# Ending the held-back weight portions earlier, and copying first partial sums by ScalarE

## The chip, the cores and the metric

One core of one Trainium2 chip runs the whole program. The metric is device time in microseconds (us) of one execution. A core has five engines, each with its own instruction queue that it works off in order: PE (TensorE, matrix products; PEld is its weight load), DVE (VectorE), ACT (ScalarE), POOL (GpSimd) and SP (SyncE, which here issues all DMAs). SBUF is the working memory, PSUM the small memory into which PE accumulates.

## The reference

Three layers follow one another. The last two are multilayer perceptrons over 2304 tokens:

```
scores = 0.125 * q @ k^T          # 4 batches, 8 heads, 576 positions, head size 64
attn   = softmax(scores where 0 <= i - j < 64)
x      = attn @ v                 # 2304 x 512
g      = x @ w_gate               # 512 x 1536
y      = (g * sigmoid(g) * (x @ w_val)) @ w_out         # 1536 x 512
h      = y @ w_in                 # 512 x 2048
out    = max(0.01 * h, h) @ w_out2                      # 2048 x 512
```

Attention, y and out are float32, the weights come as float64. The kernel multiplies in float32r with every operand split into a high and a low part, so each product is three matmuls (high*high, high*low, low*high).

## The kernel before

The first perceptron is done in six blocks of tokens (BLOCKS). Block 0 takes 24 steps, blocks 1 to 5 take 12 steps each, one for each of the 12 portions of 128 columns of d_ff. A step (`step1`, L558) is three slots long and makes twelve matmuls for the gate (pg), twelve for the value (pv) and twelve for the output of the step before (acc, in `out1`, L533). Blocks 1 to 4 have 320 tokens, block 5 has 512. FIRST holds the first slot of each block: block 1 starts at slot 72, block 5 at 216, and END is 252. The attention of each block is worked in small pieces during the block before. A slot is also the unit of priority: `prio(slot)` sets the priority of what is emitted next, and a scheduler with a cost model then puts each engine's instructions in an order, which is fixed when the program is built.

The second perceptron is a Strassen-Winograd scheme of seven products (A11, A12, S1 to S4, A22). It needs each weight portion, and four sums of parts, split into high and low. `ready2(fp)` (L319) and `ready2o(fp)` (L332) prepare one of eight portions of w_in and w_out2: two loads of 512 KB through `narrow` (L263), four sums on DVE, and four stores by `keep2` (L309) to DRAM, with two more stores at the very last portion (plain, L345). That is 16 conversions, and the list todo2 (L604) says at which slot each is emitted; the loop at L610 does so at the first step whose slot has reached it, with priority slot + 4. Of the two loads, each waits for a mark: `wait_for_mark` (L259) is a POOL instruction that copies one element of the newest g (or, later, of c) into the load's target, so that the DMA can't start earlier. All targets and stores of conversions, and the loads of x2 (below), go through one ring of three buffers (rawp).

In block 5 the kernel also builds the split right factors of the second perceptron's first pass (`x2_part`, `finish_x2`, L615 to 620) from y in DRAM, and fetches the split weights of units 0 and 1 (`fetch_a`, L623). They go into the places of weight portions that block 5 no longer needs.

The second perceptron has three passes of 768 tokens, eight units each (L751). A unit makes seven products of six matmuls each into three PSUM tiles pw, px, py (`product`, L637). ACT copies or applies the leaky function (L780, L793, L769), DVE adds (L785, L815, L826, L845, L831 to L849), POOL adds once (L816), and `halves` (L655) splits each result by an ACT cast and a POOL subtraction. The tiles t1, t5 and c lie where the first perceptron kept th and g (L775), and pw, py and px where it kept pg, pv and the attention's scores. Between the products PE makes the y matmuls of the unit before (`part_y`, L682). Their partial sums leave PSUM by `add` (L674): in the first unit of a pass by a copy (L677), in the seven others by an addition on DVE (L679). `y1`, `y2` and `y3` use the same PSUM bank one after the other, so the copy of y1 must be done before y2 can write. At the end of a pass `finish` adds the sums up and stores them from the place into which the next pass copies.

Of the kernel before, what the change touches and what calls it, by code (L numbers as in the profile page):

```python
# [22 lines left out]
def f32(ap):  # L23
    return ap.bitcast(F32)
# [3 lines left out]
def banded_attention_moe_moe(  # L28
# [12 lines left out]
    nc = tc.nc  # L41
# [17 lines left out]
    NP2 = NF2 // 2  # L59
# [19 lines left out]
    def prio(slot):  # L79

        tc.cur_priority = int(1000 * (slot + 100))
# [385 lines left out]
    for n, j in enumerate(jobs):  # L467
# [16 lines left out]
        i = n - min(jj.n for jj in jobs if jj.blk == j.blk)  # L484
# [116 lines left out]

    END = FIRST[NBLK]
    begin2, last2 = FIRST[1] + 20, FIRST[NBLK - 1]
    todo2 = [begin2 + (last2 - begin2) * i / 10 for i in range(10)] + [last2 + 3 + 5 * i for i in range(6)]  # L604
    todo2 = [(at_, (ready2, ready2o)[i % 2], i // 2) for i, at_ in enumerate(todo2)]
    for blk in range(1, NBLK):
        for f in range(NF1):
            slot = FIRST[blk] + 3 * f
            step1(slot, blk, slice(0, WIDTH[blk]), f, f == 0, f == NF1 - 1)
            while todo2 and slot >= todo2[0][0]:  # L610
                prio(slot + 4)
                _, fn, i = todo2.pop(0)
# [54 lines left out]
    def sums(r):  # L667
        return (space[10][:, 1280 * r:1280 * r + 1280] if r < 2 else space[11][:, 0:1280]).rearrange(
            "p (k n) -> p k n", k=5)

    def sums1():
        return space[11][:, 1280:2816].rearrange("p (k r n) -> p k r n", k=2, r=3)

    def add(dst, ps, first):  # L674
        prio(slot - 3)
        if first:
            nc.vector.tensor_copy(f32(dst), ps)  # L677
        else:
            nc.vector.tensor_tensor(f32(dst), ps, f32(dst), op=ALU.add)  # L679
        prio(slot)  # L680

    def part_y(n, ps, k, r, start):  # L682
        g = G[n, k]
        for m, (a, b) in enumerate(((0, 0), (0, 1), (1, 0))):
            nc.tensor.matmul(ps, lhsT=g[:, a, r * P:r * P + P], rhs=O2[n, k][:, b], start=start and m == 0,  # L685
                             stop=m == 2, skip_group_check=True)

    yb, yc = {}, {}

    def y1(n, r):  # L690
        yb[r] = ps_acc.tile([P, 2, 256], F32, tag=f"acc{r}", name="y")
        part_y(n, yb[r][:, 0], S2, r, True)
        part_y(n, yb[r][:, 1], A11, r, False)
        add(sums(r)[:, 0:2], yb[r], n % NP2 == 0)

    def y2(n, r):
        part_y(n, yb[r][:, 0], S3, r, False)
        part_y(n, yb[r][:, 1], A12, r, False)
        add(sums(r)[:, 2:4], yb[r], n % NP2 == 0)

    def y3(n, r):
        part_y(n, yb[r][:, 0], A22, r, False)
        add(sums(r)[:, 4], yb[r][:, 0], n % NP2 == 0)

    def y4(n, rs, last):
        if not last:
            yc[rs] = (ps_acc if len(rs) > 1 else ps_att).tile([P, 2, 256], F32, tag="acc3" if len(rs) > 1 else "att",
                                                              name="yc")
        for j, r in enumerate(rs):
            part_y(n, yc[rs][:, j], S4 if last else S1, r, not last and j == 0)  # L710
        add(sums1()[:, int(last), rs[0]:rs[-1] + 1], yc[rs][:, 0:len(rs)], n % NP2 == 0)

    def total(r):

# [36 lines left out]
    for n, (i, fp) in enumerate(units):  # L751
# [45 lines left out]
        for r in range(3):  # L797
            y(y1, r)
# [20 lines left out]
        y(y2, 2)  # L819
        new_o(A22, S4)  # L820
        y(y4, (0, 1), False)
        y(y4, (2,), False)
        step()
        product(n, py, S4, False)
# [23 lines left out]
        if n < LAST:  # L848
            nc.vector.tensor_tensor(t["t1"], t["t1"], t["c"], op=ALU.subtract)  # L849
            halves(n, S4, t["t1"])  # L850
        y(y4, (0, 1), True)
        y(y4, (2,), True)
        if n and (e == 0 or n == LAST):
# [34 lines left out]
```

## Time and profile before

| | |
|---|---|
| Three runs | 972.27, 975.13 and 977.71 us, median 975.13 |
| Profiled execution | 970.93 us, span 969.0 us |
| PE busy | 925.0 us (95% of the span) |
| DVE, ACT, POOL busy | 662.6, 469.0 and 336.4 us |
| Mean granted clock | 0.979 |
| Mean DMA rate | 182 GB/s, 59.0% of 16 engines' span on the main queue |

How to read it: the span is from the first to the last instruction. A busy time counts only the instructions themselves. The granted clock is the share of TensorE's full clock that the throttle allowed; 1.00 is 2.4 GHz and 0.5 is 1.2 GHz. In a list of instructions in order of time the columns are the start, the length, the engine, the line, the operation, and in square brackets the idle time of that engine just before and what ended it. Attention and block 0 fill the first 121 us, blocks 1 to 4 run to about 478 us, block 5 to about 578 us, and the rest is the second perceptron.

### The profile page before, as it was taken

Reading aid. Unit: us, or ns where it says so; the run is one execution under the profiler, and the core shown is the slowest. Engines: PE = TensorE matmul, PEld = TensorE weight load, DVE = VectorE, ACT = ScalarE, POOL = GpSimd, SP = SyncE. Lnnn points to the kernel's source line nnn. Section 1 sums busy time; section 2 is a strip of 40 time slices with the busy share of each in tenths; the row PEclk is TensorE's granted clock in tenths of the full one; section 3 lists DMA queues with packets and bytes.
Section 4 is the critical chain, followed back from the end, with each engine's and each line's share of the span. In section 5 each row is a group of like instructions: output and inputs, shape, how many; then the busy total and the mean of one; then the engine's idle time right before and its main releaser. Section 6 shows DMA issues by size and latency. Waiting matters only on the chain.

```text
span 969.0 us, 18774 instructions
## 1 busy us (share of the span) xinstructions
PE 925.0 (95%) x6573; PEld 881.5 (91%) x6573; DVE 662.6 (68%) x1554; ACT 469.0 (48%) x1194; POOL 336.4 (35%) x402
## 2 busy tenths in 40 slices
PE   8898999999999999999999984799999999999998
PEld 6788999999999999999988873799999999999997
DVE  5788842336556565665445664898998999879887
ACT  6976633335545554666333433444544445334441
POOL 1012231111111111111122121666667666576554
PEclk8999999999999999999999996899999999999999
DMA  8777621225654564554346858778557875587742
GB/s 208 220 205 226 182 43 29 74 43 157 182 163 131 140 191 131 167 155 148 112 158 231 317 188 284 269 249 261 169 184 231 262 251 165 154 252 244 252 159 83
DMA packets 193901, 176.09 MB, mean 182 GB/s; under 512 B 114576, under 2 KB 142224, under 8 KB 193808
## 3 DMA queue, kind: packets, MB, share of 16 engines
q1 hardware_dynamic: 193808, 174.90, 59.0%
q8 instruction: 52, 0.85, 0.4%
q14 instruction: 41, 0.34, 0.1%
HBM read 135.00 MB, written 39.85 MB: 180 GB/s over the span
## 4 chain that ended last, share of the span: by engine, by line
PE 73%; DMA 11%; DVE 8%; issue 2%; ACT 2%; SPq 2%; POOL 1%; POOLq 0%; DVEq 0%; ACTq 0%
PE pg L526 12%; PE y L685 12%; PE pv L526 12%; PE acc L526 12%; PE px L642 7%; PE yc L685 5%; DMA raw<-in_moe_w_gate_dram 4%; PE pw L642 4%; PE py L642 4%; PE s L202 2%; PE pv L244 2%; DMA raw<-in_moe_w_out_dram 1%; DVE u L275 1%; PE pt L233 1%; DMA raw<-in_moe_w_in_dram 1%
## 5 line engine op out<-in xcount | busy, mean ns | idle before, releaser
L579 POOL TENSOR_TENSOR g<-th,g 128x320 fp32r<-128x320 f32 (+2 forms) x84 | 81.5, 970 | 434.9 <-ACT g L578 423.3
L526 PE MATMUL pg<-x,w 128*128 128x320 f32 (+2 forms) x1008 | 175.2, 321 | 8.2 <-DVE th L569 5.2
L526 PE MATMUL pv<-x,w 128*128 128x320 f32 (+2 forms) x1008 | 174.5, 320 | 1.8 <-DVE st L219 1.2
L526 PE MATMUL acc<-g,w 128*128 128x320 f32 (+2 forms) x1008 | 170.7, 316 | 0.1
L526 PEld LDWEIGHTS pg<-x,w 128*128 128x128 f32 x1008 | 150.5, 191 | 17.0 <-DVE th L569 6.4
L526 PEld LDWEIGHTS pv<-x,w 128*128 128x128 f32 x1008 | 151.9, 192 | 9.2 <-ACT th L568 1.5
L526 PEld LDWEIGHTS acc<-g,w 128*128 128x128 f32 x1008 | 150.1, 189 | 7.0 <-POOL g L579 0.7
L685 PE MATMUL y<-space,g 128*128 128x256 f32 x1035 | 147.5, 283 | 1.0 <-DVE space L677 0.7
L685 PEld LDWEIGHTS y<-space,g 128*128 128x128 f32 x1035 | 138.3, 190 | 2.8 <-DVE space L679 1.0
L679 DVE TENSOR_TENSOR space<-y,space 128x512 f32<-128x512 f32 (+1 forms) x180 | 102.8, 593 | 11.4 <-PE y L685 10.4
L569 DVE SCALAR_TENSOR_TENSOR th<-th,pg 128x320 f32<-128x320 f32 (+2 forms) x84 | 41.3, 492 | 93.6 <-ACT th L568 93.4
L642 PE MATMUL px<-space,space 128*128 128x384 f32 x432 | 91.7, 344 | 8.2 <-DVE u L815 7.2
L664 POOL TENSOR_TENSOR g<-t,g 128x384 fp32r<-128x384 f32 x71 | 77.3, 1090 | 53.0 <-ACT g L663 48.8
L642 PEld LDWEIGHTS px<-space,space 128*128 128x128 f32 x432 | 76.3, 194 | 9.6 <-DVE u L815 7.8
L642 PE MATMUL py<-space,space 128*128 128x384 f32 x288 | 66.8, 347 | 10.1 <-ACT c L769 8.5
L578 ACT CAST g<-th 128x320 fp32r<-128x320 f32 (+2 forms) x84 | 39.1, 466 | 63.9 <-DVE th L576 63.3
L568 ACT ACTIVATE th<-pg 128x320 f32<-128x320 f32 (+2 forms) x84 | 37.0, 441 | 65.2 <-PE pg L526 63.5
L685 PE MATMUL yc<-space,g 128*128 128x256 f32 x414 | 65.0, 282 | 2.7 <-DVE space L677 2.7
L642 PE MATMUL pw<-space,space 128*128 128x384 f32 x288 | 64.7, 341 | 2.4 <-ACT c L769 1.8
L273 ACT ACTIVATE u<-raw 128x512 f32<-128x512 f32 x68 | 46.1, 682 | 41.5 <-DMA raw<-in_moe_w_out_dram 18.1
L274 DVE TENSOR_SCALAR raw<-raw 128x512 int32<-128x512 int32 x68 | 31.6, 466 | 47.9 <-DMA raw<-in_moe_w_out_dram 20.3
L664 POOL TENSOR_TENSOR g<-c,g 128x384 fp32r<-128x384 f32 x47 | 50.6, 1077 | 39.7 <-ACT g L663 29.2
(141 smaller groups left out, 1474.4 us busy)
## 6 DMA issues: line engine op xcount, KB each, us to landing
space<-o SPq DMA_DIRECT2D x147, 256.0 KB, 3.4
space<-a SPq DMA_DIRECT2D x140, 256.0 KB, 3.4
raw<-in_moe_w_out_dram SPq DMA_DIRECT2D x28, 512.0 KB, 4.3
a<-hl SPq DMA_DIRECT2D x24, 512.0 KB, 3.0
o<-hl SPq DMA_DIRECT2D x24, 512.0 KB, 2.8
raw<-in_moe_w_in_dram SPq DMA_DIRECT2D x16, 512.0 KB, 4.8
raw<-in_moe_w_gate_dram SPq DMA_DIRECT2D x12, 512.0 KB, 5.2
raw<-in_moe_w_val_dram SPq DMA_DIRECT2D x12, 512.0 KB, 4.6
```

What stands on the lines that cost most here:

```text
L202: nc.tensor.matmul(ps[:, a], lhsT=qbd[:, t, :], rhs=kT[:, w0:w0 + P], start=True, stop=True)
L273: nc.scalar.activation(u, f32(high), AF.Prelu, scale=EXP_SCALE, alpha=NEGATIVE)
L274: nc.vector.tensor_single_scalar(low, low, 29, op=ALU.logical_shift_right)
L526: nc.tensor.matmul(ps, lhsT=w(a, c), rhs=x(b, c), start=(start and n == 0), stop=(stop and n == 3 * len(cs) - 1), skip_group_check=True)
L568: nc.scalar.activation(th, pg, AF.Tanh, scale=0.5)
L569: nc.vector.scalar_tensor_tensor(out=th, in0=th, scalar=1.0, in1=pg, op0=ALU.add, op1=ALU.mult)
L578: nc.scalar.copy(g[0][:, :n], th)
L579: nc.gpsimd.tensor_tensor(g[1][:, :n], th, f32(g[0][:, :n]), op=ALU.subtract)
L642: nc.tensor.matmul(ps, lhsT=A2[n, k][:, a, c * P:c * P + P], rhs=X2[i, c, k][:, b], start=start and m == 0, stop=m == 5, skip_group_check= ...
L664: (lo or nc.gpsimd).tensor_tensor(g[:, 1], src, f32(g[:, 0]), op=ALU.subtract)
L679: nc.vector.tensor_tensor(f32(dst), ps, f32(dst), op=ALU.add)
L685: nc.tensor.matmul(ps, lhsT=g[:, a, r * P:r * P + P], rhs=O2[n, k][:, b], start=start and m == 0, stop=m == 2, skip_group_check=True)
```

## The change

Two edits. The first spreads the 16 conversions at equal distances: the step between two is 124/14 = 8.86 slots where it was 12.4 for the first ten and 5 for the last six, and the last two are due at slots 216 and 224.86 where they were due at 239 and 244. The second makes the copies of `y1` and of both `y4` calls, in the first unit of a pass, on ScalarE in place of VectorE; those of `y2` and `y3`, and all additions, stay.

```diff
     begin2, last2 = FIRST[1] + 20, FIRST[NBLK - 1]
-    todo2 = [begin2 + (last2 - begin2) * i / 10 for i in range(10)] + [last2 + 3 + 5 * i for i in range(6)]
+    todo2 = [begin2 + (last2 - begin2) * i / 14 for i in range(16)]
...
-    def add(dst, ps, first):
+    def add(dst, ps, first, copy=nc.vector.tensor_copy):
         prio(slot - 3)
         if first:
-            nc.vector.tensor_copy(f32(dst), ps)
+            copy(f32(dst), ps)
...
-        add(sums(r)[:, 0:2], yb[r], n % NP2 == 0)
+        add(sums(r)[:, 0:2], yb[r], n % NP2 == 0, nc.scalar.copy)
...
-        add(sums1()[:, int(last), rs[0]:rs[-1] + 1], yc[rs][:, 0:len(rs)], n % NP2 == 0)
+        add(sums1()[:, int(last), rs[0]:rs[-1] + 1], yc[rs][:, 0:len(rs)], n % NP2 == 0,
+            nc.scalar.copy)
```

## Rows read from the trace of the kernel before

**Rows 1.** Busy time of each engine by stretch (start and end, length, busy us and count of PE, PEld, DVE, ACT and POOL, then granted clock, DMA share, GB/s). The stretches are blocks 1 to 4 with conversions, block 5, the change to the second perceptron, the starts of passes 2 and 3, and the end.

```profile
215.00:478.00 263.00, 262.62 (x2007) 256.42 (x2006) 152.12 (x481) 142.12 (x423) 40.80 (x61) 1.00 0.52 153
478.00:571.40 93.40, 93.28 (x416) 77.38 (x416) 49.80 (x93) 33.51 (x61) 20.09 (x19) 1.00 0.60 213
571.40:614.90 43.50, 23.76 (x91) 20.69 (x90) 21.67 (x41) 18.60 (x36) 8.67 (x14) 0.73 0.83 280
726.00:756.00 30.00, 28.12 (x192) 26.92 (x191) 27.06 (x44) 12.36 (x27) 21.76 (x25) 1.00 0.78 248
858.00:873.00 15.00, 13.40 (x94) 13.13 (x93) 9.82 (x18) 4.60 (x11) 9.70 (x12) 1.00 0.89 289
944.00:969.00 25.00, 20.44 (x126) 18.39 (x124) 17.81 (x33) 4.54 (x9) 12.84 (x13) 1.00 0.24 85
```

**Rows 2.** PE in order of time at the change to the second perceptron.

```profile
574.78 3.08 PE L526 MATMUL acc<-g,w 128*128 128x512 f32 x12
577.70 1.20 PE L642 MATMUL pw<-space,space 128*128 128x384 f32 x6
578.75 1.20 PE L642 MATMUL py<-space,space 128*128 128x384 f32 x6
581.79 1.32 PE L642 MATMUL pw<-space,space 128*128 128x384 f32 x6 [1.84 <-ACT c L769]
583.67 2.29 PE L642 MATMUL pw<-space,space 128*128 128x384 f32 x6 [0.57 <-ACT t L780]
594.51 2.29 PE L642 MATMUL py<-space,space 128*128 128x384 f32 x6 [8.55 <-ACT c L769]
609.49 4.21 PE L642 MATMUL px<-space,space 128*128 128x384 f32 x12 [7.23 <-DVE u L815]
```

**Rows 3.** The chain of waits that ended last, in order of time: start, length, what.

```profile
593.75 0.19 POOL raw L261
593.96 4.22 DMA raw<-in_moe_w_out_dram
...
611.09 5.53 DMA x2raw<-x2d
```

**Rows 4.** ACT, DVE and POOL in order of time in the same stretch: the instructions that PE waited for, and what stood before them on their engine.

```profile
587.15 1.30 ACT L282 CAST hl<-sums 128x512 fp32r<-128x512 f32 x2 [3.53 <-DMA a<-hl]
593.97 0.49 ACT L769 ACTIVATE c<-pw 128x384 f32<-128x384 f32 x1 [5.51 <-POOL raw L261]
...
596.22 0.43 DVE L274 TENSOR_SCALAR raw<-raw 128x512 int32<-128x512 int32 x1 [7.04 <-DMA raw<-in_moe_w_out_dram]
597.94 0.55 DVE L785 TENSOR_TENSOR u<-px,t 128x384 f32<-128x384 f32 x1
608.89 0.55 DVE L815 TENSOR_TENSOR u<-px,t 128x384 f32<-128x384 f32 x1
...
609.52 1.00 POOL L816 TENSOR_TENSOR t<-u,t 128x384 f32<-128x384 f32 x1 [13.43 <-DVE u L815]
```

**Rows 5.** SP in order of time: loads (L269) and stores (L314) of conversions. The first two rows are the loads of the first and the tenth conversion, the third the tenth's last stores. Then come the loads of the eleventh, the loads and stores of the twelfth, and the loads of the last two.

```profile
220.74 0.97 SPq L269 DMA_DIRECT2D raw<-in_moe_w_in_dram  x2
...
453.29 0.82 SPq L269 DMA_DIRECT2D raw<-in_moe_w_out_dram  x2
...
462.62 4.65 SPq L314 DMA_DIRECT2D o<-hl  x3
...
487.71 0.94 SPq L269 DMA_DIRECT2D raw<-in_moe_w_in_dram  x2
...
504.81 0.84 SPq L269 DMA_DIRECT2D raw<-in_moe_w_out_dram  x2
512.41 5.67 SPq L314 DMA_DIRECT2D o<-hl  x4
...
573.42 1.32 SPq L269 DMA_DIRECT2D raw<-in_moe_w_in_dram  x2
...
589.62 4.68 SPq L269 DMA_DIRECT2D raw<-in_moe_w_out_dram  x2
```

**Rows 6.** All waits of PE from 215 to 478 us: who waited for whom, total, times, longest.

```profile
PE pg L526 <- DVE th L569: 0.4, 1, 0.4
```

**Rows 7.** Groups of instructions by line and shape over the whole run: the copies of the first unit of a pass, ACT copies out of PSUM, and the largest group of POOL's splits (busy us, mean ns of one, idle before).

```profile
L677 DVE COPY space<-y 128x512 f32<-128x512 f32 x18 | 11.9, 680 | 0.2 <-POOL space L718 0.2
L677 DVE COPY space<-yc 128x512 f32<-128x512 f32 x6 | 4.1, 679 | 1.5 <-DMA out_dram<-space 1.5
L551 ACT COPY ev<-acc 128x512 f32<-128x512 f32 x4 | 2.2, 581 | 0.0
L793 ACT COPY t<-py 128x384 f32<-128x384 f32 x24 | 11.4, 476 | 2.4 <-PE py L642 2.2
...
L664 POOL TENSOR_TENSOR g<-t,g 128x384 fp32r<-128x384 f32 x71 | 77.3, 1090 | 53.0 <-ACT g L663 48.8 <-issue 1.9 <-PE px L642 1.2
```

**Rows 8.** Waits from 632 to 944 us, the second perceptron without its start and end: total, times, longest.

```profile
PE yc L685 <- DVE space L677: 2.7, 2, 1.6
PE y L685 <- DVE space L677: 0.7, 2, 0.4
...
DVE space L677 <- DMA out_dram<-space: 4.6, 3, 2.0
...
ACT t L769 <- POOL t L816: 45.8, 16, 4.4
```

## The prediction

> **What bounds the kernel now.** I read the busy times by stretch first, to see where PE is not busy, then PE's own list there, then the chain of waits, then the other engines' lists. Blocks 1 to 4 are bound by PE: from 215 to 478 us it is busy for 262.62 of 263.00 us, and block 5 up to 571.4 us for 93.28 of 93.40 [rows 1]. The second perceptron in its middle is the same. What is left is the handover between them. From 571.4 to 614.9 us PE is busy for 23.76 of 43.50 us, at a mean granted clock of 0.73 [rows 1].
>
> PE's list shows where: it waits 1.84, 8.55 and 7.23 us, and after the long gaps a product of six matmuls takes 2.29 us where it took 1.20 before [rows 2]. That is the lower of the clock's two levels, 1.2 GHz where it was at 2.4.
>
> The work of that stretch, done densely at the full clock, is thirteen products of six matmuls at 1.05 us from start to start (577.70 to 578.75) and one acc group at 2.92 (574.78 to 577.70) [rows 2]: 13 x 1.05 + 2.92 = 16.6 us. These are 90 of the 91 matmuls. So 43.5 - 16.6 = 26.9 us are lost here, the largest loss in these rows.
>
> Why they are lost is in the chain of waits and in the other engines' lists. The chain runs through the last conversion: POOL's mark copy at 593.75, the load of w_out2 until 598.18, and, once the stores have left, the load of x2 for pass 2 until 616.62 [rows 3]. The stores stand between them because x2raw needs a buffer of the same ring of three. The long PE waits have two origins. The leaky c at 593.97 follows POOL's mark copy at 593.75: c is written where the mark's g lies, so it may not run before the late mark copy has read it. And DVE makes the adds L785 and L815 of unit 0 at 597.94 and 608.89, although the product into pw at 577.70 [rows 2] could only start with t1 copied out: its queue is in order and stood 7.04 us for a conversion's load first [rows 4]. POOL's add, and all that unit 0 still has to split, then waits 13.43 us for L815. None of this is data that unit 0 needs, since the conversions that run here are the last portion of each weight, which unit 7 multiplies first. It is only order on queues, a ring and one re-used place.
>
> **The edits, part by part.** *The conversions.* Their number, 16, doesn't change, so neither do their loads, stores, DVE and ACT work. What changes is where they lie. The slots at which they come out are multiples of three, so the last six come out at 219, 225, 231, 234, 240 and 246 before, and after it the last two at 216 and 225, all others in blocks 1 to 4. One falls together with the slot 225 of before, which loaded at 504.81 and had its last store issued by 518.08 [rows 5]. The last one has the two extra stores (plain), some microseconds more. So all are over some 50 us ahead of the end of block 5 (577.7), where before the last two loaded at 573.42 and 589.62 [rows 5].
>
> Gone at the handover are then the mark copy at 593.75, the wait for the load at 596.22 and those for stores on ACT. What is late next? Unit 0's own chain. PE must finish acc (577.70) and product A12 (578.9), then come c (0.49) and its cast (some 0.5): 579.9. POOL then works through seven splits and one add at 1.09 us [rows 7], 8.7 us, to 588.6; the fifth, which the first y needs with A11, is ready by 585.4. PE's dense work of 16.6 us from 571.4 lasts to 588.0. So the two nearly meet, and the lower bound of what stays lost is about 1 us. The upper bound is that both long waits stay in some form: 8.55 + 7.23 = 15.8 us [rows 2]. I take 4.6 us, what PE loses at the end of the kernel (25.00 - 20.44, at full clock [rows 1]), the nearest row of a stretch in which units run without enough y work beside them. The gain is 26.9 - 4.6 = 22.3 us, between 11.1 and 25.9.
>
> The price is paid in blocks 1 to 4. From the first conversion to the tenth are 111 slots (93 to 204) and 453.29 - 220.74 = 232.6 us [rows 5], so 2.10 us a slot; nine slots, the usual new distance, are 18.9 us. One conversion takes 14.0 us there, from its load at 453.29 to its last store at 467.27 [rows 5]. So it fits with some 5 us to spare, and the ring is free when the next one's mark copy comes; that is POOL's queue, where the subtraction L579 for acc stands behind it. SP's queue gets the same six or eight DMAs a conversion, only in front of the attention's loads at other places. DVE is busy 152.12 of 263 us there, ACT 142.12 [rows 1]; were all of it conversions, 12.4/8.86 = 1.4 times as much would be 81% and 76%. PE's matmuls are the cover. It waited 0.4 us in all for DVE in this stretch with ten conversions [rows 6]. I take 1 us lost; the bounds are 0 and the rival below.
>
> *The copies.* Three passes x (3 of y1 + 2 x 2 of y4) = 21 copies leave DVE: 9 and 6 of 512 columns at 0.68 us and 6 of half that at an estimated 0.41, together 12.7 us; on ACT one of 512 takes 0.58 and one of 384 takes 0.48 [rows 7], so some 11 us arrive. At the start of pass 2 DVE is busy 27.06 of 30 us and ACT 12.36 [rows 1], so the move goes from a crowded queue to a free one. PE waited 2.7 + 0.7 = 3.4 us for such copies [rows 8], which is the most that can be won, since the other copies were hidden by other y work. Part of it stays: the copies into sums1 wait 4.6 us in three pieces for the output DMAs of the pass before [rows 8], and that wait goes with them. Behind a waiting copy now stand the leaky functions, casts and copies of the running unit, for which POOL and then PE wait. And the copy itself may stand behind a leaky that waits for POOL, 4.4 us at the longest [rows 8]; the y2 matmuls in the same bank wait for it. So the lower end is a loss of 3 x 4.4 = 13.2 us. I take 1.0 us of gain, nearer to the waits that are there to be won, because ACT's load is less than half.
>
> The Trainium skill speaks against this edit ("TensorE: Matmul & The Clock Gate", section "Architectural detail: the array is 16× 32×32, not 1× 128×128"): ScalarE and VectorE work strictly first in, first out, and only PE can reorder, within limits. The trace agrees where DVE stands for a load with the ready L785 behind it [rows 4]. By that rule the 4.6 us of waiting for output DMAs would block the leaky functions as they now block DVE; the sum would be 949.6 us in place of 948.6, as the gain of the copies would then be nothing.
>
> *The sum*, on the profiled execution: 970.93 - 22.3 - 1.0 + 1.0 = 948.6 us. That execution is 4.2 us under the median of the runs shown, 975.13. Taking the same share off the median, 975.13 x 948.6 / 970.93 = 952.7, I forecast 952 us.
>
> **Rivals.** *Half of it*: another wait takes the handover. Block 5's result is stored only after 577.7 us, and pass 2's x2 loads need it; DVE's subtractions for pass 2 stand in its queue among unit 1's adds and wait for that load, which took 5.53 us [rows 3]. Two waits like those of now would leave 15.8 us: a gain of 11, 964 us. For it speaks that DVE and ACT are in order; against it that the ring and SP are then free.
>
> *ACT becomes the queue that holds PE*: 13.2 us lost at the pass starts, so 952 + 1 + 13 = 966 us. Against it stands ACT's low load.
>
> *Nothing is won*: the x2 load ends the chain anyway [rows 3] and PE's units wait for it; 975 us. Against it: it began at 611.09 because the ring was held, and unit 0 doesn't need it.
>
> *Slower*: with the attention beside them, conversions in blocks 2 to 4 last longer than their distance. Then the mark copy waits in POOL's queue for a ring buffer, L579 behind it, and acc behind that, which has one group of 2.92 us [rows 2] as cover. This costs from a length of 18.9 + 2.9 = 21.8 us on, and 12 such conversions of 24.5 us would cost 12 x 2.7 = 32 us, ten more than the gain: 985 us. For it: the distance shrinks by a third. Against it: the length of 14.0 us.
>
> **How the numbers follow.** Forecast 0.66, half of it 0.18, ACT 0.06, nothing 0.05, slower 0.05. The range: the forecast with a remainder of 1 us and all 3.4 us of the copies is 946; runs of before lie up to 2.9 us under their median, so 943. Upwards it takes in the half case and that of ACT: 966. Left out are nothing and slower, 0.10, and some of the edges. A difference under 0.5%, 4.9 us, can't be told from none here; faster by more is 0.66 + 0.18 + 0.06 = 0.90, within it 0.05, slower 0.05.
>
> **What would show it.** In the changed kernel's profile no load of a conversion should lie behind 520 us; PE should be granted 1.00 through the handover with less than 6 us idle between 571 and the first y matmuls; c and L815 of unit 0 should run within 5 us after acc ends; PE should stay above 99% in blocks 1 to 4; PE's waits for DVE's copies should be gone, and not replaced by waits for ACT's. The forecast is wrong if PE still has a gap over 5 us there, if the granted clock falls there, or if PE waits for th or g in blocks 1 to 4 by more than 5 us.

## The result, and the profile after

The changed kernel takes 949.47 us in the median of four runs (945.65 to 951.38), beside 973.7 us for the kernel before: a ratio of 0.9744, 95% interval 0.9695 to 0.9793. Forecast were 952 us, between 943 and 966. The profiled execution took 948.75 us with a span of 947.0 us, against 970.93 and 969.0 before, 22.2 us less. Behind line 711 the line numbers are one higher than before.

The page of the changed kernel first, busy time by engine (us, share of the span, instructions):

```profile
PE 918.7 (97%) x6573; PEld 876.9 (93%) x6573; DVE 655.8 (69%) x1533; ACT 476.3 (50%) x1215; POOL 335.8 (35%) x402
```

21 instructions have moved from DVE to ACT (1554 to 1533, 1194 to 1215), which are the copies, and PE's work is the same. The next view is the busy time by stretch, as in [rows 1]: blocks 1 to 4 with conversions, block 5 and the handover up to the end of its only wait (0.75 us).

```profile
215.00:477.65 262.65, 258.60 (x1994) 252.38 (x1990) 170.76 (x516) 150.42 (x440) 40.84 (x68) 1.00 0.64 190
477.65:584.30 106.65, 104.50 (x471) 87.19 (x470) 49.49 (x90) 34.72 (x65) 21.20 (x17) 1.00 0.48 171
584.30:605.10 20.80, 20.05 (x127) 19.85 (x126) 15.07 (x20) 14.20 (x32) 15.85 (x17) 1.00 0.94 320
```

Two things are to be seen. The handover is dense, at a granted clock of 1.00 where [rows 1] had 0.73, and PE misses 0.75 us there. But in blocks 1 to 4 PE now misses 262.65 - 258.60 = 4.05 us where it missed 0.38, and in block 5 2.15 us.

PE's list at the handover, which answers to [rows 2]:

```profile
581.38 2.92 PE L526 MATMUL acc<-g,w 128*128 128x512 f32 x12
584.15 1.23 PE L642 MATMUL pw<-space,space 128*128 128x384 f32 x6
585.21 1.20 PE L642 MATMUL px<-space,space 128*128 128x384 f32 x6
...
592.49 1.20 PE L642 MATMUL py<-space,space 128*128 128x384 f32 x6
593.53 1.23 PE L685 MATMUL yc<-space,g 128*128 128x256 f32 x9
...
601.25 1.31 PE L642 MATMUL px<-space,space 128*128 128x384 f32 x6 [0.75 <-DVE t L846]
```

After the last acc group nine products follow one another at 1.04 us, and the first y matmuls begin at 593.53 without a gap. What stood on ACT, DVE and POOL in [rows 4] is gone, in order of time (the last row is unit 1's c):

```profile
585.41 0.49 ACT L770 ACTIVATE c<-pw 128x384 f32<-128x384 f32 x1 [0.47 <-PE pw L642]
...
586.45 0.56 DVE L816 TENSOR_TENSOR u<-px,t 128x384 f32<-128x384 f32 x1 [1.86 <-PE px L642]
...
587.50 1.01 POOL L817 TENSOR_TENSOR t<-u,t 128x384 f32<-128x384 f32 x1
...
592.72 0.48 ACT L770 ACTIVATE c<-pw 128x384 f32<-128x384 f32 x1
```

The first product behind acc begins at 584.15. Unit 0's add of px comes 2.3 us after that, waiting for PE's product alone; before it came 31 us after the first product at 577.70 [rows 2, 4]. With c one has to look at the unit. Each unit makes one c, and the kernel before made its first one here:

```profile
581.23 0.50 ACT L769 ACTIVATE c<-pw 128x384 f32<-128x384 f32 x1
```

So unit 0's c came only 3.5 us after the first product before, and comes 1.3 us after it now. The c at 593.97 in [rows 4], the one behind the mark copy, is unit 1's: 16.3 us before, 8.6 us now. SP's last loads and stores of a conversion, which answer to [rows 5]:

```profile
512.35 0.84 SPq L269 DMA_DIRECT2D raw<-in_moe_w_out_dram  x2
519.82 5.68 SPq L314 DMA_DIRECT2D o<-hl  x4
526.94 0.92 SPq L314 DMA_DIRECT2D plain<-hl  x2
528.03 0.53 SPq L416 DMA_DIRECT2D x2raw<-x2d  x1
```

The conversions are over at 528 us, 56 us before block 5 ends.

What has come in is in the list of PE's waits from 215 to 585 us, the first of the two fences; the second is DVE's list of waits for the loads of conversions, 215 to 477 us. Columns: total, times, longest.

```profile
PE pv L526 <- DVE th L576: 3.1, 2, 1.6
PE pg L526 <- DVE th L569: 2.8, 2, 2.2
PE s L202 <- DVE x L252: 0.3, 1, 0.3
```

```profile
DVE raw L274 <- DMA raw<-in_moe_w_in_dram: 18.9, 11, 3.9
...
DVE raw L274 <- DMA raw<-in_moe_w_out_dram: 9.2, 7, 1.8
```

DVE stood 18.9 + 9.2 = 28.1 us for such loads. The same two lines of the kernel before are

```profile
DVE raw L274 <- DMA raw<-in_moe_w_in_dram: 5.5, 6, 1.9
DVE raw L274 <- DMA raw<-in_moe_w_out_dram: 5.0, 4, 1.6
```

together 10.5 us. One case in order of time, ACT, POOL, SP, DVE and PE of the changed kernel:

```profile
407.64 0.46 ACT L578 CAST g<-th 128x320 fp32r<-128x320 f32 x1 [1.15 <-DVE th L576]
408.24 0.88 POOL L579 TENSOR_TENSOR g<-th,g 128x320 fp32r<-128x320 f32 x1 [4.11 <-DMA o<-hl]
409.18 0.30 POOL L261 COPY raw<-g 128x1 f32<-128x1 f32 x2
...
409.64 2.12 SPq L269 DMA_DIRECT2D raw<-in_moe_w_in_dram  x2
...
413.81 0.43 DVE L274 TENSOR_SCALAR raw<-raw 128x512 int32<-128x512 int32 x1 [3.11 <-DMA raw<-in_moe_w_in_dram]
...
417.54 0.48 DVE L576 SCALAR_TENSOR_TENSOR th<-th,pv 128x320 f32<-128x320 f32 x1
...
418.07 2.02 PE L526 MATMUL pv<-x,w 128*128 128x320 f32 x12 [1.46 <-DVE th L576]
```

The load goes out behind POOL's mark copies, which follow L579. The profile names a store as what ended POOL's 4.11 us, but ACT's cast, which L579 reads, ended only at 408.10, so no hold by the ring is shown here. DVE then stands 3.11 us for the load at the head of its queue, and th, which frees the PSUM bank that pv wants, is far behind. PE waits 1.46 us.

The longest of PE's waits, 2.15 us in block 5, is of another kind:

```profile
485.20 0.62 ACT L282 CAST hl<-sums 128x512 fp32r<-128x512 f32 x1 [1.58 <-DMA o<-hl]
485.86 0.69 DVE L283 TENSOR_TENSOR hl<-sums,hl 128x512 fp32r<-128x512 f32 x1 [1.10 <-ACT hl L282]
...
487.20 3.02 PE L526 MATMUL pg<-x,w 128*128 128x512 f32 x12 [2.15 <-DVE th L569]
```

Here ACT waits for a store, since the split hl needs a buffer of the ring of three. DVE stands for ACT's cast, and th follows at 486.47. So stores hold th as well as loads.

To place the 22 us, I set four marks in both traces: the first conversion's load (220.74 before, 222.12 after), the first matmul of block 5 with 512 columns (471.78, 477.65), the end of the last acc group (577.86, 584.30), and the end. The lengths are 220.7, 251.0, 106.1 and 391.1 us before, and 222.1, 255.5, 106.7 and 362.7 after. So 28.4 us are won behind block 5, and 6.4 us given back ahead of it, 4.5 of them between the first load and block 5. The 1.4 us ahead of the first load are no effect of the edits: that mark lies between 219.37 and 222.68 us in the profiles of all kernels below in which the conversions start there.

### The profile page after: what moved, and what is told of

The parts are those of the page before. It is cut to its first block, busy times and chain, and to the rows that moved or that the text cites. A ratio compares the mean times of both kernels' runs of the same rounds, so it can differ in the third digit from the quotient of the medians.

```text
span 947.0 us, 18798 instructions
## 1 busy us (share of the span) xinstructions
PE 918.7 (97%) x6573; PEld 876.9 (93%) x6573; DVE 655.8 (69%) x1533; ACT 476.3 (50%) x1215; POOL 335.8 (35%) x402
## 4 chain that ended last, share of the span: by engine, by line
PE 65%; DMA 14%; DVE 9%; ACT 4%; issue 3%; POOL 3%; SPq 1%; POOLq 0%; DVEq 0%; ACTq 0%
PE y L685 11%; PE pv L526 10%; PE pg L526 10%; PE acc L526 10%; PE px L642 7%; PE pw L642 4%; PE yc L685 4%; PE py L642 4%; DMA raw<-in_moe_w_gate_dram 3%; DMA raw<-in_moe_w_in_dram 2%; DVE u L275 2%; PE s L202 2%; DMA o<-hl 2%; DMA raw<-in_moe_w_out_dram 1%; PE pv L244 1%
## 5 line engine op out<-in xcount | busy, mean ns | idle before, releaser
L579 POOL TENSOR_TENSOR g<-th,g 128x320 fp32r<-128x320 f32 (+2 forms) x84 | 84.0, 999 | 455.2 <-ACT g L578 428.6
L642 PE MATMUL px<-space,space 128*128 128x384 f32 x432 | 89.1, 337 | 0.8 <-DVE t L846 0.8
L642 PEld LDWEIGHTS px<-space,space 128*128 128x128 f32 x432 | 74.0, 188 | 1.6 <-DVE t L846 1.0
L274 DVE TENSOR_SCALAR raw<-raw 128x512 int32<-128x512 int32 x68 | 32.4, 476 | 48.9 <-DMA raw<-in_moe_w_in_dram 20.1
L642 PE MATMUL py<-space,space 128*128 128x384 f32 x288 | 63.1, 336 | 0.0
L642 PE MATMUL pw<-space,space 128*128 128x384 f32 x288 | 62.8, 336 | 0.0
```

Of the source, the lines that this page charges most:

```text
L274: nc.vector.tensor_single_scalar(low, low, 29, op=ALU.logical_shift_right)
L579: nc.gpsimd.tensor_tensor(g[1][:, :n], th, f32(g[0][:, :n]), op=ALU.subtract)
L642: nc.tensor.matmul(ps, lhsT=A2[n, k][:, a, c * P:c * P + P], rhs=X2[i, c, k][:, b], start=start and m == 0, stop=m == 5, skip_group_check= ...
```

## The experiments

**One edit alone.** The first kernel has the new todo2 and VectorE's copies, the second the old todo2 and ScalarE's copies; the diffs are those of the change.

> The even spacing of the 16 conversions alone, copies left on VectorE. My theory: nearly all of the gain is here; 949 to 953 us, PE idle under 3 us between the last acc group and the dense y work, and PE waits for VectorE's copies at the starts of passes 2 and 3 of about 3 us. Rival (the copies matter as much, since VectorE is crowded when unit 0 ends): over 958 us, with PE waiting for VectorE in the handover.

Measured: 950.54 us, 0.9773 (0.9744 to 0.9803). My theory holds: nearly all is in the spacing. Its profile has one gap of PE in the handover, 1.03 us for a VectorE copy, and 1.85 us of such waits at the start of pass 2, so under the forecast 3.

> The copies on ScalarE alone, conversions at the old slots. My theory: the handover stays as it was, with over 20 us lost; 971 to 975 us, a difference from before that can't be told. Rival (copies matter): 965 us or less.

Measured: 968.42 us, 0.9955 (0.9934 to 0.9977). The handover kept its gaps, but the copies won 4.6 us, more than the 0 to 2 of my theory and less than the rival's 8. The same kernel ran once more.

> The copies on ScalarE alone once more, since its time (0.9955 of before, interval 0.9934 to 0.9977) is more than my 971 to 975 us. If the copies are worth 4 us by themselves: again 0.993 to 0.998, and PE's idle time in the starts of passes 2 and 3 lies 2 us or more under before's 3.5 us, or that of the handover does. If it is the spread of runs: 0.998 to 1.002.

Measured: 968.61 us, 0.9958 (0.9939 to 0.9976), so it is no spread of runs. Where it lies isn't settled, since neither of the two signs named is there. In this profile (966.13 us) block 5 takes 104.25 us from mark to mark, 1.8 less than before, and the passes up to the end 388.4, 2.7 less; in the first run of the same kernel the profile (972.24 us) has 105.6 and 390.6. The starts of passes 2 and 3 lose 2.5 us to copies, 1 less than before. In the handover the long gaps stayed, here 9.17 and 7.15 us.

**Without the last two conversions.**

```diff
-        if fp == NP2 - 1:
+        if fp == NP2 - 2:
...
-    ... + [last2 + 3 + 5 * i for i in range(6)]
+    ... + [last2 + 3 + 5 * i for i in range(4)]
...
-    units = [(i, j if i % 2 == 0 else NP2 - 1 - j) ...
+    units = [(i, min(j if i % 2 == 0 else NP2 - 1 - j, NP2 - 2)) ...
```

> Before, with the last two conversions left out: the last portion of both weights is not prepared, and its units multiply with the portion before it. Conversions 1 to 14 keep the old slots. My theory (queues held by the two late conversions): the handover loses under 6 us in place of 27, and blocks 1 to 4 keep their PE wait of 0.4 us, so 942 to 950 us. Rival (the handover is bound by unit 0's chain or by the x2 loads of pass 2): 960 us or more, with PE gaps of over 5 us.

Measured: 942.66 us in two runs, 0.9684 (0.9641 to 0.9727). The handover is dense with the old slots of all others: the two late conversions are its loss, and neither unit 0's chain nor pass 2's x2 loads. PE waited 1.43 us in blocks 1 to 4, not the 0.4 us forecast, and 2.0 us in block 5.

**Which of their holds it is.**

```diff
-    ... p=P), True)) ...
+    ... p=P), fp < NP2 - 1)) ...
...
-    ... narrow(w2_out[f * P:f * P + P, :], True)) ...
+    ... narrow(w2_out[f * P:f * P + P, :], fp < NP2 - 1)) ...
```

> Before, with the last two conversions' loads not held by the mark copy on POOL; all data are right. If the mark copy (c must wait until it has read g's place) is the main cause: the 8.55 us wait of PE for c goes and some 10 us are won, 962 us. If the order of ACT's and VectorE's queues and the ring of three are the cause: c goes early but L785 and L815 still stand behind the conversions, at most 4 us are won, 969 to 974 us.

Measured: 973.64 us, 1.0015 (0.9994 to 1.0036): nothing won. PE's list says why:

```profile
587.90 2.29 PE L642 MATMUL py<-space,space 128*128 128x384 f32 x6 [0.58 <-ACT c L769]
...
601.60 2.29 PE L642 MATMUL px<-space,space 128*128 128x384 f32 x6 [8.55 <-DVE u L785]
612.02 3.72 PE L642 MATMUL px<-space,space 128*128 128x384 f32 x12 [6.62 <-DVE u L815]
```

The wait for unit 1's c has shrunk from 8.55 to 0.58 us, as it should without the mark copy, and a wait of the same 8.55 us for L785 has taken its place. DVE still stands 7.97 us for the last conversion's load, until 598.51, and makes L785 behind it at 600.99. The load itself was no earlier: its two halves were sent at 591.54 and 596.29 us, the second after 2.2 us of waiting for a store, where before they went out from 589.62 [rows 5]. So taking the mark away alone wins nothing, because the late load holds DVE's queue in any case. Two things were not taken apart: this order of the queue, and a second ring of three (up), from which the conversions and the adds L785 and L815 both take their target u.

**The price in blocks 1 to 5.** The first attempt leaves the loads where they are and moves the work behind them one step later.

```diff
+            while rest:
+                prio(slot + 1)
+                next(rest.pop(0), None)
...
+        yield
+        x, y = (two(narrow_rest(raw, True)) for raw in raws)
...
+        if late:
+            wait_for_mark(u[:, 0:1])
+        shifted = high if late else low
```

> The changed kernel, with each conversion's loads issued at its slot as now and its ACT and VectorE work held by a second mark copy on POOL from the next step (some 5 to 6 us later, when the load of 4.6 us has landed). The shift writes over the element that ACT has read, so that VectorE's first instruction comes after ACT's. My theory of the price in blocks 1 to 5 (VectorE stands in order for a load with th behind it): PE's waits for th of 5.9 us between 215 and 585 us fall under 2 us, 943 to 947 us. Rival (the price is VectorE's load itself, or the ring): the waits stay, 948 to 953 us.

Measured: 945.45 us, 0.9712 (0.9686 to 0.9738). Block 5's wait of 2.15 us went, but the waits from 215 to 585 us only fell to 4.6 us, so the experiment didn't do what it was made for and tells little. Its own list shows that the edit didn't get the distance it needed:

```profile
279.63 0.31 POOL L261 COPY raw<-g 128x1 f32<-128x1 f32 x2 [1.65 <-DMA inb<-in_k_dram]
...
282.91 0.30 POOL L261 COPY u<-g 128x1 f32<-128x1 f32 x2
...
284.81 0.43 DVE L283 TENSOR_SCALAR raw<-raw 128x512 int32<-128x512 int32 x1 [3.42 <-ACT u L281]
```

The second mark copy came 3.3 us after the first, and the load, sent at 279.84 us, wasn't there before 284.1. DVE stood for it as before, only by way of ACT, 50.0 us in all up to 477 us, more than the changed kernel's 28.1.

The others change the distance and the place of the conversions:

```diff
-    todo2 = [begin2 + (last2 - begin2) * i / 14 for i in range(16)]
+    todo2 = [begin2 + 9.4 * i for i in range(16)]      # first
+    todo2 = [FIRST[1] + 10.2 * i for i in range(16)]   # second
+    todo2 = [48 + 11.8 * i for i in range(16)]         # third, also worked off in block 0
```

> The changed kernel with 9.4 slots between conversions in place of 8.86: the last two come out at slots 225 and 234 in place of 216 and 225, at the places of the old twelfth and fourteenth. If all that counts is that the last conversion's stores are issued before block 5 ends, 947 to 951 us, with no gap of PE over 2 us in the handover. If the ring shared with the x2 loads pushes the last one past the end of block 5 (the old fourteenth loaded at 553.5 us and stored until 573), 955 us or more.

Measured: 945.18 us, 0.972 (0.9695 to 0.9745), a little better than expected. The last two conversions load at 508.92 and 536.43 us, the last store is issued by 558.6, and PE has no gap in the handover at all. So the conversions can end some 30 us later than the changed kernel's (528) and still leave the handover dense. DVE stood 32.9 us for loads before 478 us, longer than in the changed kernel, and yet PE's waits from 215 to 585 us were 5.1 us, of them 1.8 for th. How long DVE stands doesn't by itself say how long PE waits, then. The time can't be told from the changed kernel's, as the intervals overlap.

> The changed kernel, the first conversion due at slot 72 in place of 92 and 10.2 slots between two in place of 8.86, the last at slot 225 as now. If the price in blocks 1 to 4 comes from the density of the conversions (a load must wait for a ring buffer of the one before, and VectorE then stands for it): PE's waits from 215 us to the end of block 5 fall from 6 us to 3 us, 945 to 948 us. If it comes from the conversions that lie beside block 5's double attention, whatever the distance: they stay at 5 us or more, 948 to 952 us.

Measured: 940.25 us, 0.9666 (0.9641 to 0.969), better than either theory said. PE's waits for DVE from 119 to 585 us, and DVE's for loads from 119 to 478:

```profile
PE pv L526 <- DVE th L576: 0.3, 1, 0.3
PE pg L526 <- DVE th L569: 0.2, 1, 0.2
...
DVE raw L274 <- DMA raw<-in_moe_w_out_dram: 8.7, 6, 2.6
DVE raw L274 <- DMA raw<-in_moe_w_in_dram: 8.6, 9, 1.7
```

The end of the conversions is where the change put it and block 5's attention lies where it lay. The distance grew, from 9 slots to 9 to 12, and the start moved into block 1, with 14 of the 16 conversions still ahead of block 5. In the same stretches DVE's waits for loads fell from 30.7 us (2.6 of them end between 477 and 478 us) to 17.3, and PE's from 6.4 to 0.5 us. That is 5.9 of the 9.7 us between the two profiled spans; the rest isn't placed.

> The changed kernel, the first conversion due at slot 48, in block 0, and 11.8 slots between two, the last at slot 225 as now; nearly the distance of before (12.4). Density theory: PE's waits for VectorE in blocks 1 to 5 fall to 2 us or less, and VectorE's waits for loads there to under 15 us from 28; 942 to 946 us. Rival (place, not distance): waits of 4 us or more stay, 947 to 951 us.

Measured: 942.37 us, 0.9688 (0.9662 to 0.9714). PE waited 0.9 us, as the theory said, and the time is in its range; DVE's 16.8 us for loads from 119 us on (12.2 from 215) miss its 15. The intervals of the second and the third overlap. Both runs speak for the distance and against the place beside block 5's attention. They don't show it in full: each new list makes the scheduler order all engines anew, and the first of the three, at 9.4 slots, kept most of PE's waits. What part the ring of three has wasn't tried either: a ring of four was not run.

**The copies, once the handover is dense.** The early start with the old `add`:

> The early start (slot 72, 10.2 slots) with the copies left on VectorE: what the copies are worth once the handover is dense. If they win 4 us here as they did alone: 943 to 946 us. If their gain alone came from VectorE's crowded queue in the disturbed handover, and 1 us from the starts of passes 2 and 3: 940 to 943 us.

Measured: 941.26 us, 0.9683 (0.9665 to 0.97), 1.0 us behind the early start with ScalarE's copies, and the intervals overlap. What the copies won alone is mostly gone where the conversions are out of the way.

The version with the early start and ScalarE's copies has the lowest median found, 33 us under the kernel before; its interval lies just under the changed kernel's 0.9695 to 0.9793.

## Why the prediction was right

*The handover.* Forecast: 26.9 us lost, 4.6 stay, 22.3 won. Measured: 0.75 us of PE's idle time stay, and from the end of the last acc group to the end 28.4 us are won. The cause is confirmed by leaving the last two conversions out, which also shows that unit 0 needs no data of theirs. Of the holds the run without the mark shows that the late load is enough without the mark copy. The prediction did not see whose c waited: the c at 593.97 is unit 1's, and unit 0's came 3.5 us behind acc already before, so the sign it named for unit 0's c could not tell the kernels apart. The term was mis-sized in the remainder: I took the end of the kernel, 4.6 us, as the nearest row, but the end has no next unit to fill in with, and here PE had products of three units. My own lower bound, 16.6 us of dense PE work against a POOL chain to 585.4 for the first y, was the better guide. The gain went past my upper end of 25.9, which left out a wait of 0.98 us at 621.34 and what the copies won.

*Blocks 1 to 4.* Forecast: 1 us lost. Measured: PE's waits from 215 us to the end of block 5 went from 0.4 us, and 1.0 more in block 5, to 6.2, and the stretch from the first load to block 5 is 4.5 us longer. This is the step that was furthest off. I had taken one conversion, 14.0 us, for all, and asked only whether it fits into 18.9 us. In the changed kernel the one that loads at 452.30 has its last store issued at 469.21, 16.9 us. Above all I had not asked what stands behind the load on DVE: L274 waits at the head of the queue with th behind it, and so does L283 where its buffer's store is late (2.15 of the 6.2 us). The mechanism of my *slower* rival, a mark copy that waits for the ring in front of L579, isn't shown: of POOL's 40 waits ahead of L579 from 215 to 478 us, 39 end with ACT's cast, and at 408 us L579 could not start earlier for its cast either.

*The copies.* Forecast: 1.0 us won. Beside the new spacing they are worth 950.54 - 949.47 = 1.1 us, and 1.0 beside the early start, within intervals that overlap; the size is borne out, not proved. PE's waits for copies and the splits at pass starts, from 632 us on, fell from 3.4 us to 1.9 for copies (1.5 for DVE's, 0.4 for ACT's) and 0.7 for a split. ACT stood 5.8 us for output DMAs in place of DVE's 4.6, and no leaky made PE wait, so the rival in which ACT becomes the queue that holds PE didn't come. PE's waits for DVE's copies didn't all go, as the signs had it: the copies of y2 and y3 stay on DVE, and 1.5 us of waits with them. The sum by the rule of the Trainium skill ("TensorE: Matmul & The Clock Gate", section "Architectural detail: the array is 16× 32×32, not 1× 128×128"), 949.6 us on the profiled execution, can't be told from 948.6. That the copies alone win 4.4 us was not foreseen.

*Half of it, nothing.* Both are out. The x2 loads for pass 2 stand ahead of unit 1's add L846, as the half case said, and cost 0.75 us.

So the sum, 948.6 us on the profiled execution against 948.75 measured, and 952 against 949.47 in the medians, came out so near by luck: two errors of opposite sign, 4 to 6 us each, nearly cancelled. What was right is the mechanism at the handover. The range held the time. Of the signs for blocks 1 to 4 one failed, PE at 98.5% in place of 99%; the other held, as PE waited 3.7 us for th there where I had named 5. For block 5, where the 2.15 us came on top, I had named none.

## What to carry to other kernels

Preparation that is held back until it collides with a change of stage costs more than its own work, because queues keep the order that was planned for it: look for the first instruction of the new stage that is ready and not run, and read what stands ahead of it on its engine. If one hold is taken away, ask whether a second one of the same length stands behind it, before crediting the first. When work is packed more densely into a saturated stretch, don't ask only whether its busy time fits: see what stands in the in-order queue behind each instruction that waits for a load or a store, and whether the saturated engine needs it soon. Starting the work earlier, with the same end, took the time from 0.9744 to 0.9666 of the kernel before.

## What the runs showed of the hardware that was not expected

A product of six matmuls took 2.29 us after PE had waited 8.55 us, against 1.20 before, and the granted clock of the whole handover was 0.73; with the gap gone it stayed at 1.00. So the handover of [rows 1] lost more than PE's idle time there, 43.50 - 23.76 = 19.7 us: the same 23.76 us of busy time would be about 16.6 at the full clock, 7 less, by the prediction's estimate of dense work. A copy of 512 columns out of PSUM took 0.59 us on ACT (15 of them) and 0.68 on DVE (9 left), which is by itself too little for any of the differences above.
